# V projections of a fused attention and spectral-filter kernel placed straight behind the K projections of their x block

## The chip, the cores and the metric

The kernel runs on one core of a Trainium2 chip. A core has a TensorE for matmuls (PE in the profile; its weight loads are PEld), a VectorE (DVE), a ScalarE (ACT), a GpSimd (POOL) and a SyncE (SP), which here only issues DMAs. Matmuls write to PSUM, eight banks of 128 x 512 float32 values; everything else lies in SBUF. The metric is the device time of one execution in microseconds, and lower is better.

## The reference

Two independent halves are computed and joined along the last axis: a spectral filter on `A_x`, and softmax attention with 32 heads of 20 channels on `B_x`. Sequence length 2048, model width 640, bf16.

```
def _A_ref(x, w_r, w_i):                 # x (1, 2048, 640)
    X = rfft2(x as float32); X = X * (w_r + 1j * w_i)
    return irfft2(X).astype(bfloat16)
def _B_ref(x, wqkv, wo):                 # 32 heads, 20 channels each
    q, k, v = split(x @ wqkv)
    p = softmax(q @ k.T * 20 ** -0.5)
    return (p @ v) @ wo
return concatenate([a, b], axis=-1)
```

## The kernel before, in words

**A planner that writes the order.** The program is built by a list scheduler in the kernel file. The class `KB` holds work of several kinds, steps a clock of its own (`self.now`, in ns, with a planned duration for each operation), and at each step gives each engine the best thing that its own books show as ready. What comes out is a fixed instruction order for each engine, with semaphore waits put in where data or buffers need them. The planned times are not measured times; on the chip each engine simply follows its list.

**Attention.** There are 32 units (`UNITS`): a block of 512 queries (`qc`) and a group of four heads (`g`). A unit has 64 score tiles: 16 key tiles (`kt`, 128 keys each) times four heads (`j`). Unit 0 is query block 0 with head group 0, unit 1 is query block 1 with head group 0, units 2 and 3 are head group 1, and so on. A score tile is a matmul with 32 rows of the array (line 808), transposed: keys on the partitions, 512 queries along the free axis.

- ScalarE takes two tiles at once, out of a set of two PSUM banks (banks 0,1 and 2,3 in turn), and writes exp into one slot of a ring of seven slots (line 1389). A slot is free again when both its tiles have been multiplied by V.
- VectorE takes other tiles, four to a batch, and works out exp by arithmetic on the bits of float16 (lines 933, 961, 962, 963). It takes none before 30 us of planned time (`EARLY`, `MAXE`).
- P·V (line 1048) adds 21 x 512 per head into one PSUM bank for a unit. One column of V is ones, which gives the sums of the softmax.

TensorE's choice at each planned step is `step_pe1`: first the next two score tiles for ScalarE (`try_act_fill`); then P·V if at least eight tiles wait, or if the ring is full; then background groups (`try_bg`). A background group may start only if there is room before ScalarE would run dry, and only one is in work on TensorE at a time; its matmuls ("chunks") may be interleaved with scores. As long as ScalarE has not begun (`act_started` is False) or no score tile is ready, the room is unlimited. Background groups use PSUM banks 4 to 7, and all eight banks before ScalarE has begun.

**The background groups of the front** (`jobs_B`). x comes in four blocks of 512 rows (`i` or `kc`), and the smaller the priority number the earlier a group goes, if it is ready:

| group | line | matmuls | planned | priority |
|---|---|---|---|---|
| transposes of x block `i`, four groups | 584 (eviction 590) | 20 of 128 columns | 240 or 360 ns each group | 10 i + t2 |
| K of head group 0, block kc | 606 (eviction 614) | 5 of 512 | 1080 ns | 10 kc + 5 |
| Q(0,0), query block 0 of head group 0 | 606 (614) | 5 of 512 | 1080 ns | 5.5 |
| V of heads 0 to 7, two x tiles `2*k2`, `2*k2+1` | 682 (eviction 688) | 10 of 160 | 700 ns | 500 + k2 |
| Q(0,1), query block 1 of head group 0 | 606 (614) | 5 of 512 | 1080 ns | 550 |
| K and Q of head group 1 | 606 (614) | 5 of 512 | 1080 ns | 605 to 650 |
| K and Q of the other heads ("packed") | 635 (eviction 647) | 5 of 512 | 1080 ns | 1000 and up |

A transpose's eviction may run on ScalarE before the first scores and on VectorE at any time; K and Q are evicted by VectorE. A K block holds four key tiles, so it feeds 16 score tiles of a unit; two V groups together cover the key tiles of one block. Score tiles are taken in order, and no later unit is begun while the present one has tiles that aren't ready, except by VectorE.

Loads are issued by SyncE in this order: identity, x block 0 in two halves, the K and Q weights of head groups 0 and 1, a bias, and then, once the first half of x has landed, x block 1, the V weights, x blocks 2 and 3, the remaining K weights and the remaining Q weights.

**What else runs.** When all of x is transposed, GpSimd begins to fold `A_x` for the spectral filter (lines 1588 to 1595, eight rounds), and its results go through DRAM. The filter's matmuls (lines 1688, 1745, 1833, 1860) are released by planned times between 200 and 770 us and fill TensorE's gaps beside the attention. After a unit, its sums go through DRAM, GpSimd multiplies (line 1100), and the output projection (line 1194) follows when a query block is complete.

Of the kernel before, what the change touches and what calls it, by code (L numbers as in the profile page):

```python
# [293 lines left out]
class KB:  # L294
# [275 lines left out]
    def jobs_B(self):  # L570
        ps, psb = self.ps, self.psb
        J = {}
        for i in range(4):
            for t2 in range(2):
                for gi, cbs in enumerate(((0, 1, 2), (3, 4))):
                    n = len(cbs)
                    pe = []
                    for ci, c in enumerate(cbs):
                        for tt in range(2):
                            def mk(bank, ci=ci, c=c, tt=tt, i=i, t2=t2):  # L580
                                o = psb[:, bank, (ci * 2 + tt) * 128:(ci * 2 + tt) * 128 + 128]
                                in_ = self.xn[i][:, 2 * t2 + tt, c * 128:(c + 1) * 128]
                                idn = self.ident
                                return lambda e: e.transpose(o, in_, idn)
                            pe.append((mk, 60.0, [("xn", i, 2 * t2 + tt), ("ident",), ("xz", i), ("z", "D", 0)]))

                    def mkev(bank, cbs=cbs, n=n, i=i, t2=t2):
                        o = self.xT[:, cbs[0]:cbs[0] + n, i * 512 + t2 * 256: i * 512 + t2 * 256 + 256]
                        in_ = psb[:, bank, 0:n * 256].rearrange("p (c s) -> p c s", c=n)
                        return lambda e, en: (e.copy(o, in_) if en == "act" else e.tensor_copy(o, in_))  # L590
                    ev = [(mkev, 0.52 * n * 256 + 70, [("z", "A", 0)], [("xT", i, t2, gi)], [], True)]
                    J[("xT", i, t2, gi)] = Job("xT", 10.0 * i + t2, pe, ev)

        def xk(i):
            return [("xT", i, t2, gi) for t2 in range(2) for gi in range(2)]
# [31 lines left out]
        def packed(which, c, kc, sb, free):  # L627
            pe = []
            col = which * 640
            for cc in range(5):  # L630
                def mk(bank, cc=cc):
                    o = ps[:, bank, :]
                    l = self.wqkv[:, cc, col + c * 128: col + (c + 1) * 128]
                    r_ = self.xT[:, cc, kc * 512:(kc + 1) * 512]
                    return lambda e: e.matmul(o, l, r_, start=(cc == 0), stop=(cc == 4))  # L635
                wks = []
                if 128 * c < 160:
                    wks.append((("wq0", "wk0")[which],))
                if 128 * c + 128 > 160:
                    wks.append((("wq", "wk")[which],))  # L640
                pe.append((mk, 216.0, wks + [("z", "B", 0), ("z", "A", 0)] + xk(kc) + (free if cc == 0 else [])))

            def mkev(bank):
                o = self.stg[sb][:, kc * 512:(kc + 1) * 512]
                in_ = ps[:, bank, :]
                sc = (QSCALE, 1.0)[which]
                return lambda e, en: e.tensor_scalar(o, in_, sc, None, ALU.mult)  # L647
            ev = [(mkev, 610.0, [("z", "C", 0)], [("stg", which, c, kc)], [("stgb", sb, kc)], False)]
            return Job("pk%d" % which, 0.0, pe, ev)
# [3 lines left out]
        for n_, (which, c) in enumerate(order):  # L653
# [3 lines left out]
                for kc in (range(2, 4) if (which, c) == (0, 0) else range(4)):  # L657
                    j = packed(which, c, kc, sb, free)
# [12 lines left out]
        for m in range(4):  # L671
            for k2 in range(8):
                pe = []
                for i in range(2):
                    kt = 2 * k2 + i
                    for c in range(5):
                        def mk(bank, c=c, kt=kt, i=i, m=m):
                            o = ps[:, bank, i * 160:(i + 1) * 160]
                            l = self.xT[:, c, kt * 128:(kt + 1) * 128]
                            r_ = self.wqkv[:, c, 1280 + m * 160: 1280 + (m + 1) * 160]  # L680
                            st = (c == 0 and i == 0)
                            return lambda e: e.matmul(o, l, r_, start=st, stop=(c == 4), skip_group_check=True)  # L682
                        pe.append((mk, 70.0, [("wv",), ("z", "B", 0), ("z", "A", 0)] + xk(kt // 4)))

                def mkev(bank, k2=k2, m=m):
                    o = self.V[:, 2 * k2:2 * k2 + 2, m, 0:168].rearrange("p k (h e) -> p k h e", e=21)[:, :, :, 0:20]
                    in_ = ps[:, bank, 0:320].rearrange("p (k h e) -> p k h e", k=2, h=8)
                    return lambda e, en: (e.copy(o, in_) if en == "act" else e.tensor_copy(o, in_))  # L688
                ev = [(mkev, 405.0, [], [("V", m, 2 * k2), ("V", m, 2 * k2 + 1)], [], True)]
                j = Job("V", 500.0 + k2 if m == 0 else 1000.0 + 20.0 * m - 5 + k2 * 0.1, pe, ev)  # L690
                j.rel = 0.0 if m == 0 else self.VJ0 + self.VJ1 * (m + 0.125 * k2)
                J[("V", m, k2)] = j
        for j in J.values():
# [587 lines left out]
    def try_bg(self, room):  # L1281
        if any(J.nxt < len(J.pe) for J in self.flight):
            return False
        banks = self.POOLB if self.act_started and self.ua < NU else (4, 5, 6, 7, 0, 1, 2, 3)
        if self.act_started and not self.tail() and (self.n_dve_banks() >= len(self.POOLB) - 1 or (self.want_pv() and sum(1 for b in self.POOLB if self.bank_owner[b] is None) < 2)):
            return False
        best = None
        for J in self.jobs:
            if not J.pe or not self.eligible(J):
                continue  # L1290
            if best is not None and (best.prio, best.seq) <= (J.prio, J.seq):
                continue
            if min(sum(c[1] for c in self.part(J)), self.BMIN) + self.SW > room or not self.ready(J):
                continue
            best = J
        if best is None:
            return False
        fb = best.bank
        for b in banks if fb is None else ():
            if self.bank_owner[b] is None and self.P.peek("pe", w=[("ps", b)]) <= self.now:  # L1300
                fb = b
                break
        if fb is None:
            return False
        self.jobs.remove(best)
        best.bank = fb
        self.bank_owner[fb] = "bg"
        self.flight.append(best)
        self.emit_chunk(best)
        return True  # L1310
# [799 lines left out]
```

## Time and profile before

| | before |
|---|---|
| time, median of 3 runs | 796.37 us (796.0 to 797.88) |
| profiled execution, span | 797.3 us |
| mean granted TensorE clock | 0.998 |
| exponentials on ScalarE (two tiles each) | 823 |
| score tiles on VectorE | 403 |
| DMA traffic, mean | 61 GB/s |

The page of the profile gives the busy time of each engine as a share of the span, the chain of work that ended last, and the costliest groups of instructions with the idle time before them and who ended it. The timeline gives instructions in order of time, merged where the same line repeats; a bracket at the end tells how long the engine sat idle before it, and which engine and line ended the wait. TensorE's busy time is taken from matmul durations that overlap, so a stretch can look full while more would fit in. The windows view gives, for a stretch of time, the busy time of each engine, the granted clock and the DMA traffic.

### The profile page before, as it was taken

The numbers are of one execution on the slowest core, as the hardware profiler recorded it, in microseconds if no ns is written. First come the engines' busy times: TensorE is split into PE (matmuls) and PEld (weight loads), VectorE is DVE, ScalarE is ACT, GpSimd is POOL, SyncE is SP. The second block draws the span as 40 slices with busy tenths as digits, with TensorE's granted clock in tenths as the row PEclk, the third lists the DMA queues.
The fourth block names the chain that finished last, engine by engine and source line by source line (L and its number), as shares of the span: only waits on it lengthen the run. The fifth ranks groups of instructions, "written<-read, shape, count | busy, mean of one in ns | idle before, by whom it ended". The sixth has DMA issues, their size and how long they took to land.

```text
span 797.3 us, 15245 instructions
## 1 busy us (share of the span) xinstructions
PE 763.8 (96%) x6107; PEld 239.3 (30%) x6107; DVE 698.2 (88%) x1079; ACT 765.1 (96%) x836; POOL 138.7 (17%) x141
## 2 busy tenths in 40 slices
PE   8999999999989999999999999999998999999997
PEld 4422424233222222233233332222222322322333
DVE  4687899889998998999999999989899889989884
ACT  5789999999999999999999999999999999999995
POOL 7895800000100012103013010000000000000000
PEclk9999999999999999999999999999999999999999
DMA  9213221030154112212012112020200102111101
GB/s 296 79 44 104 82 72 46 23 69 20 45 159 153 59 64 60 70 44 57 6 36 61 44 36 107 19 72 19 72 20 16 35 30 73 52 36 35 51 21 53
DMA packets 42860, 48.65 MB, mean 61 GB/s; under 512 B 16454, under 2 KB 36168, under 8 KB 41760
## 3 DMA queue, kind: packets, MB, share of 16 engines
q1 hardware_dynamic: 42016, 46.32, 19.4%
q0 software_dynamic: 768, 1.32, 0.6%
q8 instruction: 49, 0.80, 0.4%
q14 instruction: 27, 0.22, 0.1%
HBM read 32.53 MB, written 8.36 MB: 51 GB/s over the span
## 4 chain that ended last, share of the span: by engine, by line
ACT 74%; PE 16%; DVE 8%; SPq 1%; issue 0%; DMA 0%
ACT arena L1389 74%; PE ps L808 5%; PE ps L1048 3%; DVE arena L962 2%; DVE arena L933 2%; PE ps L1688 1%; PE ps L606 1%; DVE arena L961 1%; PE ps L1194 1%; PE ps L635 1%; PE ps L1745 1%; PE ps L682 1%; DVE arena L963 1%; PE ps L564 1%; SPq L472 1%
## 5 line engine op out<-in xcount | busy, mean ns | idle before, releaser
L1389 ACT ACTIVATE arena<-ps 128x1024 f16<-128x1024 f32 x823 | 757.8, 1118 | 15.3 <-PE ps L1048 9.8
L808 PE MATMUL ps<-arena 32*128 32x512 bf16 x2048 | 324.6, 385 | 23.5 <-ACT arena L1389 18.8
L933 DVE TENSOR_SCALAR arena<-ps 128x512 int16<-128x512 f32 x403 | 269.7, 684 | 46.0 <-PE ps L808 42.8
L1048 PE MATMUL ps<-arena 128*32 128x512 f16 x2451 | 211.6, 385 | 1.4 <-DVE arena L963 0.7
L808 PEld LDWEIGHTS ps<-arena 32*128 32x128 bf16 x2048 | 79.5, 91 | 321.6 <-ACT arena L1389 299.0
L1100 POOL TENSOR_TENSOR arena<-arena 128x512 bf16<-128x512 f32 x30 | 41.7, 1391 | 543.4 <-DMA arena<-rd 543.4
L962 DVE TENSOR_TENSOR arena<-arena 128x2048 f16<-128x2048 f16 (+2 forms) x102 | 129.9, 1274 | 2.2
L961 DVE TENSOR_SCALAR arena<-arena 128x2048 uint16<-128x2048 uint16 (+2 forms) x102 | 73.9, 725 | 1.9
L963 DVE TENSOR_SCALAR arena<-arena 128x2048 uint16<-128x2048 uint16 (+2 forms) x102 | 73.6, 722 | 0.4
L1048 PEld LDWEIGHTS ps<-arena 128*32 128x32 bf16 x2451 | 45.9, 94 | 87.7 <-issue 65.9
L1833 PE MATMUL ps<-arena 128*128 128x512 bf16 (+1 forms) x192 | 56.8, 386 | 0.0
L635 PE MATMUL ps<-arena 128*128 128x512 bf16 x170 | 50.0, 384 | 0.3 <-DVE arena L688 0.3
L1688 PE MATMUL ps<-arena 128*128 128x512 bf16 x160 | 46.8, 384 | 0.9 <-DVE arena L933 0.9
L1745 PE MATMUL ps<-arena 128*128 128x322 bf16 (+1 forms) x198 | 38.0, 303 | 0.2 <-DVE arena L1776 0.2
L1860 PE MATMUL ps<-arena 128*128 128x320 bf16 (+1 forms) x192 | 37.1, 303 | 0.4 <-DVE arena L933 0.3
L1776 DVE TENSOR_TENSOR arena<-ps,arena 128x644 bf16<-128x644 f32 (+1 forms) x34 | 27.9, 822 | 3.7 <-PE ps L1745 3.1
L682 PE MATMUL ps<-arena 128*128 128x160 bf16 x320 | 30.5, 234 | 0.0
L1194 PE MATMUL ps<-arena 128*128 128x320 bf16 (+1 forms) x152 | 28.4, 302 | 0.1
L1079 DVE COPY arena<-ps 128x512 f32<-128x512 f32 (+1 forms) x33 | 21.9, 667 | 5.5 <-PE ps L1048 5.5
L647 DVE TENSOR_SCALAR arena<-ps 128x512 bf16<-128x512 f32 x34 | 23.3, 684 | 3.1 <-PE ps L635 3.1
L682 PEld LDWEIGHTS ps<-arena 128*128 128x128 bf16 x320 | 21.1, 98 | 11.3 <-issue 10.1
L688 DVE CAST arena<-ps 128x320 bf16<-128x320 f32 x32 | 15.4, 485 | 6.1 <-PE ps L682 6.0
(72 smaller groups left out, 361.3 us busy)
## 6 DMA issues: line engine op xcount, KB each, us to landing
arena<-ct SPq DMA_DIRECT2D x8, 1024.0 KB
arena<-rd SPq DMA_DIRECT2D x120, 64.0 KB
out_dram<-arena SPq DMA_DIRECT2D x32, 160.0 KB
arena<-arena SPq DMA_DIRECT2D x42, 80.0 KB
arena<-in_A_x_dram SPq DMA_DIRECT2D x16, 160.0 KB
xs<-arena SPq DMA_DIRECT2D x16, 160.0 KB
arena<-xs SPq DMA_DIRECT2D x2, 1280.0 KB
arena<-arena SPq DMA_DIRECT2D x105, 20.0 KB
```

The source lines that it names most:

```text
L635: return lambda e: e.matmul(o, l, r_, start=(cc == 0), stop=(cc == 4))
L682: return lambda e: e.matmul(o, l, r_, start=st, stop=(c == 4), skip_group_check=True)
L808: return e.matmul(self.ps[:, bank, :], self.KT[32 * j:32 * j + 32, g, kt * 128:(kt + 1) * 128], self.QT[32 * j:32 * j + 32, g, qc * 512:(q ...
L933: return e.tensor_scalar(o, in_, 0.0, 31744.0, ALU.max, ALU.min)
L961: (lambda e, en: e.tensor_scalar(Gu, Iu, 0x3FF, 0x3800, ALU.bitwise_and, ALU.bitwise_or), 100 + 0.26 * 512 * n, ik, [("G", b), ("G2", b)], ...
L962: (lambda e, en: e.tensor_tensor(Gf, If, Gf, ALU.mult), 125 + 0.52 * 512 * n, ik + [("G", b)], [("G2", b)], [], "p3"),
L963: (lambda e, en: e.tensor_scalar(Iu, Iu, 0x7C00, 0x0008, ALU.bitwise_and, ALU.bitwise_or), 100 + 0.26 * 512 * n, [("G2", b)], ik, [], "p4"),
L1048: inst = e.matmul(self.ps[32 * j:32 * j + 32, bank, :], v_, p_, start=s_, stop=False, tile_position=(0, 32 * j), skip_group_check=True)
L1389: self.put("act", lambda e: e.activation(o, in_, AF.Exp, bias=ACT_BIAS, scale=ACT_SCALE), 0.8333 * 512 * n + 60.0, r=[("ps", b) for b in b ...
L1688: return lambda e: e.matmul(o, l, r_, start=(t == 0), stop=(t == 7))
L1745: return lambda e: e.matmul(o, lhs, r_, start=st, stop=sp)
L1833: return lambda e: e.matmul(o, l, r_, start=(n == 0), stop=(n == 7))
```

## The change

The change touches two places of the planner and no instruction's form. The V groups for heads 0 to 7 get priorities between those of the K group of their x block and of the next block's transposes: 7.0 and 7.1 for block 0, 17.2 and 17.3 for block 1, 27.4 and 27.5, 37.6 and 37.7. They serve the first units' P·V, which empties the ring of exponentials. The second place is the choice of background groups: from the moment that Q(0,0) has begun until the first scores have been issued, groups with more than 400 ns of planned matmuls are passed over, so that none of them stands in front of the first scores.

```
@@ -687,7 +687,7 @@
                     in_ = ps[:, bank, 0:320].rearrange("p (k h e) -> p k h e", k=2, h=8)
                     return lambda e, en: (e.copy(o, in_) if en == "act" else e.tensor_copy(o, in_))
                 ev = [(mkev, 405.0, [], [("V", m, 2 * k2), ("V", m, 2 * k2 + 1)], [], True)]
-                j = Job("V", 500.0 + k2 if m == 0 else 1000.0 + 20.0 * m - 5 + k2 * 0.1, pe, ev)
+                j = Job("V", 10.0 * (k2 // 2) + 7.0 + k2 * 0.1 if m == 0 else 1000.0 + 20.0 * m - 5 + k2 * 0.1, pe, ev)
                 j.rel = 0.0 if m == 0 else self.VJ0 + self.VJ1 * (m + 0.125 * k2)
                 J[("V", m, k2)] = j
         for j in J.values():
@@ -1287,6 +1287,8 @@
         best = None
         for J in self.jobs:
             if not J.pe or not self.eligible(J):
+                continue
+            if not self.act_started and self.jB[("Q0", 0, 0)].nxt and sum(c[1] for c in J.pe) > 400:
                 continue
             if best is not None and (best.prio, best.seq) <= (J.prio, J.seq):
                 continue
```

More of the change, by code (lines that the diff above doesn't have):

```diff
@@ L689, in jobs_B @@
                 ev = [(mkev, 405.0, [], [("V", m, 2 * k2), ("V", m, 2 * k2 + 1)], [], True)]
-                j = Job("V", 500.0 + k2 if m == 0 else 1000.0 + 20.0 * m - 5 + k2 * 0.1, pe, ev)
+                j = Job("V", 10.0 * (k2 // 2) + 7.0 + k2 * 0.1 if m == 0 else 1000.0 + 20.0 * m - 5 + k2 * 0.1, pe, ev)
                 j.rel = 0.0 if m == 0 else self.VJ0 + self.VJ1 * (m + 0.125 * k2)
@@ L1289, in try_bg @@
             if not J.pe or not self.eligible(J):
+                continue
+            if not self.act_started and self.jB[("Q0", 0, 0)].nxt and sum(c[1] for c in J.pe) > 400:
                 continue
```

## The prediction

> **What bounds the kernel now.** I read the page's busy times first, then the chain that ended last, then ScalarE's timeline for the first 60 us, then TensorE's for the stretch in which ScalarE stands still, and last the windows of the granted clock.
>
> From the page, the busy shares and the start of the chain by engine and line:
>
> ```profile
> PE 763.8 (96%) x6107; PEld 239.3 (30%) x6107; DVE 698.2 (88%) x1079; ACT 765.1 (96%) x836; POOL 138.7 (17%) x141
> ...
> ACT 74%; PE 16%; DVE 8%; SPq 1%; issue 0%; DMA 0%
> ```
>
> ScalarE (ACT) carries three quarters of the chain. TensorE's 96% is no second bound: the mean matmul of 512 columns stands at 385 ns, but ten of them on L606 below take 2.33 us, so the next starts after (2.33 - 0.38) / 9 = 0.216 us; the ends overlap. ScalarE is idle for 797.3 - 765.1 = 32.2 us in all, and its timeline says where the early part of that lies (start, length, what; in brackets the idle time before and who ended it):
>
> ```profile
> 13.58 6.52 ACT L1389 ACTIVATE arena<-ps 128x1024 f16<-128x1024 f32 x7 [0.82 <-PE ps L808]
> 24.82 24.44 ACT L1389 ACTIVATE arena<-ps 128x1024 f16<-128x1024 f32 x26 [4.71 <-PE ps L1048]
> 49.67 1.02 ACT L1389 ACTIVATE arena<-ps 128x1024 f16<-128x1024 f32 x1 [0.41 <-PE ps L808]
> 51.96 1.02 ACT L1389 ACTIVATE arena<-ps 128x1024 f16<-128x1024 f32 x1 [1.27 <-PE ps L808]
> 54.23 6.52 ACT L1389 ACTIVATE arena<-ps 128x1024 f16<-128x1024 f32 x7 [1.24 <-PE ps L1048]
> ```
>
> Seven exponentials run, exactly the seven slots of the P ring, and then ScalarE waits 4.71 us for a P·V matmul (L1048) to empty a slot. P·V needs V. TensorE's timeline shows when V came:
>
> ```profile
> 8.69 2.33 PE L606 MATMUL ps<-arena 128*128 128x512 bf16 x10
> 10.86 1.28 PE L584 MATMUL ps<-arena 128*128 128x128 bf16 x20
> 11.98 1.24 PE L606 MATMUL ps<-arena 128*128 128x512 bf16 x5
> ...
> 18.65 0.82 PE L606 MATMUL ps<-arena 128*128 128x512 bf16 x3
> 19.40 0.39 PE L808 MATMUL ps<-arena 32*128 32x512 bf16 x2
> 19.72 0.61 PE L606 MATMUL ps<-arena 128*128 128x512 bf16 x2
> 20.26 0.39 PE L808 MATMUL ps<-arena 32*128 32x512 bf16 x2
> 20.58 0.73 PE L584 MATMUL ps<-arena 128*128 128x128 bf16 x10
> 21.17 1.56 PE L682 MATMUL ps<-arena 128*128 128x160 bf16 x20
> 22.57 1.24 PE L606 MATMUL ps<-arena 128*128 128x512 bf16 x5
> 23.74 1.04 PE L1048 MATMUL ps<-arena 128*32 128x512 f16 x14
> ```
>
> The first V (L682) stands at 21.17, behind all transposes (L584) and three K groups of unit 0; another K group follows, and only then P·V. The five matmuls at 11.98 are a K group of head group 1: the last evictions of the transposes just issued were still running, so the K block of x block 1 could not be meant. It stands in front of the first scores at 13.15.
>
> A third fact, from the windows (length, busy PE, PEld, DVE, ACT, POOL, granted clock, DMA share, GB/s):
>
> ```profile
> 50.50:53.50 3.00, 3.00 (x10) 0.49 (x8) 1.19 (x3) 1.22 (x2) 3.00 (x4) 0.50 0.01 3
> ```
>
> TensorE ran this stretch at half clock, and ScalarE lost the 0.41 + 1.27 + 1.24 = 2.9 us around it.
>
> **What the Trainium skill says.** "TensorE: Matmul & The Clock Gate", section "Back-to-back issue gap", gives N / 2.4 + 2.5 ns between warm matmuls: 216 ns at 512 columns, as worked out above. The same page, "What's actually happening", says that the clock falls to half after an idle window of about 3.4 us; the trace agrees with the length (half clock for some 3.4 us), and no run yet shows what counts as idle. "SBUF — State Buffer", section "SBUF: two separate sides", says that VectorE and GpSimd lock one port pair against each other for a whole instruction; the trace agrees: the multiply L962 takes 2.30 us at 35.50 and 45.25, beside GpSimd's fold, and 1.22 us after 100 us.
>
> **The change, part by part.** *The priorities of V for heads 0 to 7.* They go from 500 + k2 to 7, 17, 27, 37 for the pairs of x blocks 0 to 3, so each pair runs behind the K group (5, 15, 25, 35) of its block and ahead of the next block's transposes (10, 20, 30). No instruction is added or removed. The first pair cannot run before its weights are there; that load is fourth in a queue of 0.69 + 0.41 + 0.66 + 0.82 = 2.6 MB, and the traffic by microsecond sums to 2.4 MB at 10 us and 2.8 MB at 11, so it lands near 11 us (an estimate). The planner books its bytes at 270 per ns from a 4.0 us issue and another 1.9 us, about 12.2 us. V therefore does not wait for data, and it comes behind the first scores, near 13.5 us.
>
> *What that frees.* Twenty V matmuls start to start take 22.57 - 21.17 = 1.4 us; in the 0.6 us that a pair of scores leaves per exponential (starts 0.93 apart, 0.32 of it for scores) they are done after three exponentials. Eight tiles are then multiplied by V after the fourth, before the ring's seven slots are full. The 4.71 us goes.
>
> *The rule against long groups.* Between the first matmul of Q(0,0) and the first scores no group planned at over 400 ns starts: K, Q and V groups (1080 and 700 ns) wait, transposes do not. This removes the K group at 11.98. The scores still need a PSUM bank that ScalarE's transpose eviction frees at 11.40 + 1.37 = 12.77. So from 13.15 the first scores can move to 12.8 at the earliest: 0 to 0.4 us, I take 0.2.
>
> *What it moves to the front instead.* K for tiles 32 to 63 now queues behind V and P·V. TensorE's demand up to the last K block of unit 0: V of three blocks 6 x 0.7 = 4.2; three K groups 3 x 1.08 = 3.2; 40 transposes 2.2 (20 are 1.12 start to start); P·V for 24 exponentials, six batches of eight matmuls at about 0.5, 3.0: 12.7 us. Supply: the block must be complete some three exponentials ahead (two sets filled ahead, one eviction of 0.75), so 21 x 0.61 = 12.8 us. It balances with nothing left for groups that can't be split, turns that hold no whole chunk, and waits for evictions. A tenth lost is 1.3 us. Walking the list in order I find the K block of tile 32 about 0.9 us late; for tile 48 the walk gives anything between on time and 3.5 us late. I take 1.5 us of new ScalarE waits, with 0.9 and 4.4 as ends.
>
> *What costs nothing.* Moving the group at 11.98 and Q(0,1) back: head group 1 is due only at tile 128, and 44 tiles are done near 37 us, so some 30 us lie before it. V's evictions (0.49 us each) on VectorE: it is busy 3.9 of the 6.5 us from 13.6 to 20.1.
>
> *What shifts.* The last transposes move from 21 us to about 33, and GpSimd's fold, which waits for them, with them. Two of its eight rounds lay before the first VectorE batch of four score tiles; they now lie beside later ones. A batch beside the fold took 0.85 + 2.30 + 1.22 = 4.4 us against 2.6 alone; one more such batch costs VectorE 1.8 us, part of which is idle time. I take 0, and 0.5 us of end time as the other bound.
>
> *From ScalarE time to end time.* ScalarE does 823 x 2 = 1646 of the 2048 tiles, VectorE the rest from 30 us on, which the change does not move. A microsecond of ScalarE saved at the front is worth 1646 / 2048 = 0.80 us at the end. Sum: (0.2 + 4.7 - 1.5) x 0.80 = 2.7 us, so 796.4 - 2.7 = 793.7 us.
>
> **The rivals.** *The half-clock stretch goes too.* It followed stretches in which TensorE stood idle (48.0 to 48.3, 49.9 to 50.3) behind slow VectorE evictions. With one K group more left over there is more for TensorE at that time; against it, the fold still slows VectorE there. Worth 2.9 x 0.80 = 2.3: 791.4 us.
>
> *A wait that takes the place of the one removed.* If the last transposes and their evictions come behind V and behind the first VectorE score tiles at 30 us, the K block for tile 48 comes 3.5 us late, the new waits are 4.4 us, and (0.2 + 4.7 - 4.4) x 0.80 = 0.4 remains: 796.0 us. For it speaks that demand and supply of TensorE balance so closely; against it, that ScalarE's own wait gives TensorE full speed.
>
> *Slower.* TensorE starves in a new place (the whole list is planned anew from the first microsecond), a second half-clock stretch costs 2.3, and the later fold 0.5: 796.0 + 2.8 = about 799 us. For it: a stretch of this kind exists already, and later exponentials show scattered waits of up to 1.4 us per 10 us. Against it: ScalarE sits at 10.00 of 10 us in most windows from 110 to 780, so there is little that can get worse.
>
> **How the numbers follow.** The forecast 0.32, without the half-clock stretch 0.20, the wait moved 0.28, slower 0.20. A change of 0.3% is 2.4 us, so faster holds the first two, 0.52; same 0.28; slower 0.20. The range reaches from below the second case, 790.0, with 1.4 us for what else moves, to 798.5, past the third, and leaves out most of the slower case.
>
> **What would show it.** Right: the first L682 close behind the first scores near 13.5; no ScalarE idle time of over 2 us ended by L1048 before 30 us; the first exponential near 13.4; small waits ended by L808 at about 28 and 36 us; the fold's start near 33 us. Wrong: a wait of 3 us or more for L808 before unit 0 ends (the rival of the moved wait), or V waiting for its weights, or ScalarE's idle time after 40 us grown by more than 2 us.

## The result, and the profile after

| | before | after |
|---|---|---|
| time, median of 5 runs each | 797.07 us (796.0 to 798.48) | 806.33 us (805.05 to 809.12) |
| ratio, with its 95% interval | | 1.0117 (1.0092 to 1.0143) |
| profiled execution, span | 797.3 us | 803.2 us |
| exponentials on ScalarE | 823 | 829 |
| score tiles on VectorE (L933) | 403 | 392 |

The kernel became 1.2% slower. Lines past 1289 have moved by two: the exponential is now L1391, the filter's first matmul L1690. From the page of after, the busy times, the chain by engine and the two rows that do the exponentials (the last column is the idle time before them and what ended most of it):

```profile
PE 756.5 (94%) x6052; PEld 239.5 (30%) x6105; DVE 689.2 (86%) x1059; ACT 771.5 (96%) x842; POOL 145.2 (18%) x141
...
ACT 52%; PE 39%; DVE 7%; issue 1%
...
L1391 ACT ACTIVATE arena<-ps 128x1024 f16<-128x1024 f32 x829 | 764.2, 1105 | 15.0 <-PE ps L808 10.8
...
L933 DVE TENSOR_SCALAR arena<-ps 128x512 int16<-128x512 f32 x392 | 262.2, 683 | 61.3 <-PE ps L808 58.5
```

ScalarE stands idle for 803.2 - 771.5 = 31.7 us, nearly as long as before, 32.2 us. What the change won at the front was thus lost again elsewhere. And ScalarE is busy for 6.4 us more (771.5 against 765.1), since it has six exponentials more to do where VectorE did eleven tiles fewer. These two terms make up the 5.9 us between the two profiled executions; the medians lie further apart, by 9.3 us, because the profiled execution of after was its fastest, and that of before (799.17 us) was slower than all five of its runs. TensorE's share of the chain rose from 16% to 39%; in e3 below, which is faster than before, it is 27%, so the share alone says little.

The front itself went largely as foreseen. TensorE's timeline of after shows V straight behind the first scores:

```profile
12.83 0.39 PE L808 MATMUL ps<-arena 32*128 32x512 bf16 x4 [0.68 <-ACT arena L590]
13.16 1.14 PE L682 MATMUL ps<-arena 128*128 128x160 bf16 x14
```

And ScalarE's timeline of after:

```profile
13.26 14.77 ACT L1391 ACTIVATE arena<-ps 128x1024 f16<-128x1024 f32 x16 [0.48 <-PE ps L808]
29.03 6.10 ACT L1391 ACTIVATE arena<-ps 128x1024 f16<-128x1024 f32 x7 [1.00 <-PE ps L808]
38.36 6.52 ACT L1391 ACTIVATE arena<-ps 128x1024 f16<-128x1024 f32 x7 [3.23 <-PE ps L808]
45.52 1.02 ACT L1391 ACTIVATE arena<-ps 128x1024 f16<-128x1024 f32 x1 [0.64 <-PE ps L808]
46.77 30.93 ACT L1391 ACTIVATE arena<-ps 128x1024 f16<-128x1024 f32 x33 [0.23 <-PE ps L808]
```

The wait of 4.71 us for a P·V is gone. Waits for scores of 1.00, 3.23 and 0.64 us, 4.9 us together, stand in its place; but the half-clock stretch at 50 us is gone too (the windows of after give a granted clock of 1.00 from 50.5 to 53.5 us). So up to 100 us after is ahead; e4 below shows that most of this lead can be chance. Where it falls behind is seen by counting: two tiles for each exponential on ScalarE and one for each L933 on VectorE, from the windows view of these two rows, each window from 0 to the time given.

| tiles done by | 60 us | 100 | 120 | 200 | 240 | 260 | 400 | 500 | 780 |
|---|---|---|---|---|---|---|---|---|---|
| before | 97 | 196 | 252 | 470 | 581 | 634 | 1012 | 1271 | 2037 |
| after, against before | +5 | +9 | +3 | -3 | -1 | -8 | -15 | -14 | -16 |

Before does 2037 / 780 = 2.6 tiles per us, so 16 tiles are 6.1 us, which is the difference of the two spans (5.9). Two stretches carry it: 100 to 200 us, and from 240 to 400 us. Both lie far from the edit.

### The profile page after: what moved, and what is told of

Same layout as the page of the kernel before. It is cut to its first block, busy times and chain, and to the rows that moved or that the text cites. A ratio compares the mean times of both kernels' runs of the same rounds, so it can differ in the third digit from the quotient of the medians.

```text
span 803.2 us, 15169 instructions
## 1 busy us (share of the span) xinstructions
PE 756.5 (94%) x6052; PEld 239.5 (30%) x6105; DVE 689.2 (86%) x1059; ACT 771.5 (96%) x842; POOL 145.2 (18%) x141
## 3 DMA queue, kind: packets, MB, share of 16 engines
q1 hardware_dynamic: 42016, 46.32, 19.1%
## 4 chain that ended last, share of the span: by engine, by line
ACT 52%; PE 39%; DVE 7%; issue 1%
ACT arena L1391 51%; PE ps L808 14%; PE ps L1048 9%; PE ps L635 4%; PE ps L682 3%; PE ps L1835 2%; DVE arena L933 2%; PE ps L1690 2%; DVE arena L962 2%; PE ps L606 1%; PE ps L1194 1%; PE ps L1862 1%; DVE arena L961 1%; DVE arena L963 1%; PE ps L1747 1%
## 5 line engine op out<-in xcount | busy, mean ns | idle before, releaser
L1391 ACT ACTIVATE arena<-ps 128x1024 f16<-128x1024 f32 x829 | 764.2, 1105 | 15.0 <-PE ps L808 10.8
L808 PE MATMUL ps<-arena 32*128 32x512 bf16 x2048 | 323.6, 385 | 27.1 <-ACT arena L1391 22.7
L933 DVE TENSOR_SCALAR arena<-ps 128x512 int16<-128x512 f32 x392 | 262.2, 683 | 61.3 <-PE ps L808 58.5
L808 PEld LDWEIGHTS ps<-arena 32*128 32x128 bf16 x2048 | 79.4, 91 | 323.3 <-ACT arena L1391 302.1
L1100 POOL TENSOR_TENSOR arena<-arena 128x512 bf16<-128x512 f32 x30 | 44.9, 1498 | 548.1 <-DMA arena<-rd 548.1
L962 DVE TENSOR_TENSOR arena<-arena 128x2048 f16<-128x2048 f16 (+1 forms) x99 | 126.8, 1280 | 1.9
L963 DVE TENSOR_SCALAR arena<-arena 128x2048 uint16<-128x2048 uint16 (+1 forms) x99 | 74.4, 751 | 0.2
L961 DVE TENSOR_SCALAR arena<-arena 128x2048 uint16<-128x2048 uint16 (+1 forms) x99 | 72.1, 729 | 2.1
L1835 PE MATMUL ps<-arena 128*128 128x512 bf16 (+1 forms) x176 | 52.8, 386 | 2.4 <-issue 1.6
L635 PE MATMUL ps<-arena 128*128 128x512 bf16 x155 | 46.0, 383 | 2.5 <-issue 1.8
L1690 PE MATMUL ps<-arena 128*128 128x512 bf16 x144 | 43.1, 387 | 3.7 <-issue 3.6
```

Source lines behind the costliest of these rows:

```text
L808: return e.matmul(self.ps[:, bank, :], self.KT[32 * j:32 * j + 32, g, kt * 128:(kt + 1) * 128], self.QT[32 * j:32 * j + 32, g, qc * 512:(q ...
L933: return e.tensor_scalar(o, in_, 0.0, 31744.0, ALU.max, ALU.min)
L961: (lambda e, en: e.tensor_scalar(Gu, Iu, 0x3FF, 0x3800, ALU.bitwise_and, ALU.bitwise_or), 100 + 0.26 * 512 * n, ik, [("G", b), ("G2", b)], ...
L962: (lambda e, en: e.tensor_tensor(Gf, If, Gf, ALU.mult), 125 + 0.52 * 512 * n, ik + [("G", b)], [("G2", b)], [], "p3"),
L963: (lambda e, en: e.tensor_scalar(Iu, Iu, 0x7C00, 0x0008, ALU.bitwise_and, ALU.bitwise_or), 100 + 0.26 * 512 * n, [("G2", b)], ik, [], "p4"),
L1391: self.put("act", lambda e: e.activation(o, in_, AF.Exp, bias=ACT_BIAS, scale=ACT_SCALE), 0.8333 * 512 * n + 60.0, r=[("ps", b) for b in b ...
```

## The experiments

All ratios are against the kernel before, run beside it on the same chip (its medians there: 798.35 to 798.9 us). A "draw" is the list that the planner happens to write, and a "redraw" another one, got by moving a planned number that means nothing for the work. Below, "first pair", "priorities" and "rule" are parts of the change, put into the kernel before.

### The parts of the change, and a redraw of the kernel before

Four runs. The rule alone and the priorities alone are the two hunks of the change. The first pair gives the early priority to the two V groups of x block 0 only:

```
# e3_first_pair, against before
-  Job("V", 500.0 + k2 if m == 0 else ...
+  Job("V", (7.0 + k2 * 0.1 if k2 < 2 else 500.0 + k2) if m == 0 else ...
# e4_before_other_latency: a planned latency of the kernel before, and nothing else
-    L_DVE = 140.0
+    L_DVE = 141.0
```

> The rule against long groups alone, V priorities as before. Theory A (the front's new order itself costs: V pushes the K groups and the fold back): 0 to -0.5 us against before, since V stays where it was, and 400 to 406 score tiles on VectorE. Theory B (any edit of the front makes the planner write another list for the following 700 us, and the list of before is a favourable one among many): +2 to +9 us, though the first 60 us are nearly unchanged. Theory C (the K group of head group 1 that the rule takes out of an idle stretch is missed later): +3 us or more, and the loss shows in TensorE waits before 120 us.

> The V priorities alone, without the rule. Theory A: as the changed kernel, +8 to +10 us, with the waits for scores near 28 and 36 us. Theory B: the same gain of tiles at 90 us as the changed kernel (about 8), and an end anywhere from 0 to +9 us. Theory C: 0 us or faster.

> Only the two V groups of x block 0 go ahead (priorities 7.0 and 7.1), the other six stay at 500 and up, no rule. Theory A: the 4.7 us wait goes and no wait for scores of over 1 us comes in its place, the fold starts before 30 us, and the kernel is 3 to 6 us faster than before. Theory B: ahead by 8 to 14 tiles at 90 us, but an end of -4 to +5 us, because the rest of the list is new. Theory C: faster by 3 us or more, since the K group of head group 1 stays in its place.

> The kernel before with one planned figure changed: the planner books a VectorE result 141 ns after its end in place of 140. No priority and no rule is touched. Theories A and C: within 1 us of before, 400 to 405 score tiles on VectorE. Theory B: +2 to +9 us, fewer score tiles on VectorE than 403, tile counts equal to before's within 3 up to 60 us.

| | time, us | ratio (95%) | tiles against before at 100 | 200 | 260 | 780 us |
|---|---|---|---|---|---|---|
| e1 rule alone | 806.24 | 1.0111 (1.0063 to 1.0160) | +7 | -4 | -4 | -12 |
| e2 priorities alone | 799.72 | 1.0027 (1.0013 to 1.0040) | +10 | +4 | +5 | 0 |
| e3 first pair | 793.40 | 0.9945 (0.9928 to 0.9962) | +20 | +14 | +16 | +11 |
| e4 redraw of before | 800.90 | 1.0033 (1.0017 to 1.0049) | +7 | +5 | +7 | -6 |

Three things follow. In these four runs the slow-down is in the rule: alone it costs about what the whole change does, and the priorities, with the same front as after (waits of 1.00 and 3.23 us), end 0.27% above before. Second, the later V groups are what breaks the front. ScalarE's timeline of e3 shows no wait for a K block:

```profile
13.34 13.86 ACT L1389 ACTIVATE arena<-ps 128x1024 f16<-128x1024 f32 x15 [0.82 <-PE ps L808]
29.20 18.49 ACT L1389 ACTIVATE arena<-ps 128x1024 f16<-128x1024 f32 x20 [2.01 <-PE ps L1048]
47.86 33.10 ACT L1389 ACTIVATE arena<-ps 128x1024 f16<-128x1024 f32 x36 [0.17 <-PE ps L1048]
```

One pair of V groups sets P·V going; the other three blocks' V stay behind the K groups, and one wait of 2.01 us for the ring is left. e3 does 829 exponentials and 392 tiles on VectorE, just as after does, in 11 us less: the smaller share of VectorE is not by itself what makes a kernel slow. It has a price, though. VectorE does 388 to 396 tiles in all twelve kernels here with V early, and 398 to 405 in seven of the eight with V as before (394 in e10). In e2 ScalarE stands idle for 3.8 us less than in before (28.4 against 32.2) and is busy for 3.7 us more (768.8 against 765.1), so nothing is left of the gain. Why VectorE falls behind with V early is not shown.

Third, e4 changes nothing at the front and one number by 0.7%, and takes 0.33% longer. The list that the planner draws is new behind the first place that differs, and the one in the kernel before is a good draw. In e4 that place lies late: the order of TensorE's weight loads, by line, is that of before up to 387 us, and e4 is 3 tiles ahead of before at 400 us and 6 behind at 780. Its 7 tiles at 100 us are therefore not of the list. Its first exponential came at 12.99 us and not at 13.58, and it has no half clock at 50 us, where the same list in before has (the line of before stands in the prediction):

```profile
50.50:53.50 3.00, 3.00 (x30) 0.84 (x28) 2.48 (x5) 2.41 (x3) 3.00 (x3) 1.00 0.01 3
```

A count of tiles from one profile against that of before thus carries some 7 tiles of chance, and of the 9 that after is ahead at 100 us few are sure.

### How much is the draw: the same kernels with another start of the filter

`FT0` is the planned time at which the filter's matmuls begin to be released. It is moved by 0.1 or 0.3 us; the front stays as it is in each kernel. The order of TensorE's weight loads stays too, up to 390 us in e5, 326 in e6, 336 in e7 and 392 in e8.

```
-    FT0 = 200000.0
+    FT0 = 200100.0     # e5 (after), e7 (before)
+    FT0 = 200300.0     # e6 (rule alone), e8 (first pair)
```

> The changed kernel with one planned figure of the filter changed: its first group is released at 200.1 us of planned time in place of 200.0. The order up to about 200 us is the changed kernel's own. Theory A' (the change and above all its rule lose the time at the front, before 200 us): 804 to 808 us, as the changed kernel. Theory B (the loss is in the list that the planner happens to write for the later part): the tile counts at 160 us are the changed kernel's within 2, and the end differs from it by 2 us or more, probably downward, 799 to 804 us, since the changed kernel lies at the slow end of the lists seen so far.

> The rule alone, with the filter's first release at 200.3 us of planned time. Theory C (the rule itself costs): 804 to 808 us, as the rule alone. Theory B: 798 to 804 us, with more than 3 us between this and the rule alone, tile counts equal up to about 200 us.

> The kernel before with the filter's first release at 200.1 us of planned time in place of 200.0. Theories A' and C: within 1 us of before. Theory B: +1 to +6 us against before, with an order equal to before's up to about 200 us, and fewer score tiles on VectorE than 403.

> Only the first pair of V groups ahead, no rule, with the filter's first release at 200.3 us of planned time. Theory A': 792 to 795 us, as the first pair alone, since the front is the same. Theory B: slower than the first pair alone by 1 to 8 us, 795 to 801 us.

| | time, us | ratio (95%) |
|---|---|---|
| e5 after | 810.85 | 1.0125 (1.0060 to 1.0189) |
| e6 rule alone | 801.72 | 1.0038 (1.0023 to 1.0052) |
| e7 before | 801.29 | 1.0041 (1.0025 to 1.0057) |
| e8 first pair | 800.64 | 1.0034 (1.0018 to 1.0051) |

A tenth of a microsecond in a planned time costs the kernel before 0.41%, and 0.3 us takes the whole gain of the first pair away: e8 is +12 tiles ahead at 400 us, as e3 is, and 3 behind at 780. A difference of 0.3 or 0.4% between two lists is therefore no sign that the edit between them does anything. After stays 1.2% slower, but e5 has its list up to 390 us, so what after loses before that, e5 loses too; it is no second draw of that part. The rule alone doesn't stay 1.1% slower, so something in e1 is not the rule itself.

Nor is all of a difference the list. Each run has a mean granted clock of its own, and of the twenty runs of e7 the five at 0.997 or more have a median of 799.25 us, where such runs of before have 798.14: 0.14% of the 0.41%. The rest goes with half clock (last section).

### The filter's first matmul stands before its data

TensorE's timeline of after around 240 us:

```profile
238.76 0.39 PE L808 MATMUL ps<-arena 32*128 32x512 bf16 x2 [0.53 <-ACT arena L1391]
241.14 0.71 PE L1690 MATMUL ps<-arena 128*128 128x512 bf16 x2 [1.99 <-issue]
241.78 0.61 PE L808 MATMUL ps<-arena 32*128 32x512 bf16 x2
242.32 1.03 PE L1690 MATMUL ps<-arena 128*128 128x512 bf16 x2
```

TensorE stands for 1.99 us before the first matmul of the filter's first stage, and all scores queued behind it stand too; and the two L1690 behind the next scores take 1.03 us, where such a pair takes 0.59 to 0.60 us in e9. After's profile names no releaser ("issue"). The timeline of e1 has a wait at the same matmul and names it, a load of a table of constants; that after waits for the same load is an inference:

```profile
236.63 0.82 PE L1690 MATMUL ps<-arena 128*128 128x512 bf16 x3 [1.36 <-DMA arena<-ct]
```

The planner books these loads at 270 bytes per ns. If the books are too fast, slower books should put the matmul later and take the stand away:

```
# e9_after_later_filter, against after: planned rate of the filter's two loads
-        rate = 90.0 if name == "spread" else 270.0
+        rate = 90.0 if name == "spread" else 215.0 if name in ("ld_xA", "ld_tab") else 270.0
```

> The changed kernel, with the filter's x and table loads booked by the planner at 215 bytes per ns in place of 270, so that the filter's first matmuls stand about 2 us later in TensorE's list and find their table landed. The order up to about 235 us is the changed kernel's. Theory D (the changed kernel loses about 10 tiles between 238 and 260 us, because TensorE stands 2 us before the filter's first matmul, and then runs at half clock): no wait of over 0.5 us ahead of L1690's first matmul, no half-clock stretch between 238 and 250 us, 52 tiles or more between 240 and 260 us where the changed kernel has 44, and 801 to 804 us. Theory B alone (chance of the later list): tile counts at 240 us equal, and any end from 799 to 810 us.

It took 803.19 us, ratio 1.0050 (1.0034 to 1.0066), where after had 1.0117. The windows view (length, busy PE, PEld, DVE, ACT, POOL with their counts, granted clock, DMA share, GB/s), first of after:

```profile
238.00:241.50 3.50, 0.99 (x7) 0.32 (x5) 1.93 (x5) 2.54 (x3) 0.00 (x0) 1.00 1.00 354
241.50:245.00 3.50, 3.50 (x20) 0.58 (x18) 1.90 (x3) 2.05 (x2) 0.00 (x0) 0.52 1.07 430
240.00:260.00 20.00, 18.56 (x127) 4.78 (x134) 14.45 (x22) 17.28 (x20) 1.26 (x1) 0.91 0.34 125
```

then of e9:

```profile
238.00:241.50 3.50, 2.97 (x28) 0.76 (x25) 3.21 (x5) 3.50 (x5) 0.00 (x0) 1.00 0.96 345
241.50:245.00 3.50, 3.50 (x28) 1.01 (x28) 3.21 (x7) 3.50 (x5) 0.00 (x0) 1.00 1.09 434
240.00:260.00 20.00, 20.00 (x156) 5.14 (x155) 18.24 (x29) 20.00 (x23) 1.26 (x1) 1.00 0.34 127
```

The DMA engines are full in both (share about 1.0), so the loads come no sooner. In e9 TensorE works through scores meanwhile, ScalarE has no idle time from 240 to 260 us, and the clock stays at 1.00. In after TensorE is busy 0.99 of 3.5 us, and the next 3.5 us run at a granted clock of 0.52. This is the idle window of which the Trainium skill speaks ("TensorE: Matmul & The Clock Gate", section "What's actually happening"); the trace of after agrees with it, though TensorE was not idle for the whole of the window. How idle a window must be the runs don't show: the stand of 1.63 us in e14 was followed by no half clock, and other half-clock stretches followed shorter stands (last section). At 260 us e9 is 9 tiles ahead of after, at 780 us 5 tiles. The times differ by 0.67% of after's 1.17%; since e9 is a redraw as well, a part of that can be the draw. After in another draw, e16 below, stands there for 0.88 us only and comes to 1.0059, close to e9.

e5, with after's list up to there, has the same stand, 1.88 us, and 10.2 us of half clock behind it. In the three kernels with the rule alone (e1, e6, e14) it is 1.36, 1.48 and 1.63 us, and the clock stays at 1.00 there. None of the eleven kernels without the rule stands there longer than 1.02 us (before: 0.86). That the rule leads to longer stands by more than the draw is not shown: e12 and e18 below have the rule and stand under 0.3 us.

### The later fold

In after GpSimd begins the fold at 33.02 us and ends it near 110, where before began at 21.49 and ended near 97. From 100 to 120 us before has no GpSimd at all beside VectorE, after has 9.3 us, and VectorE did 12 tiles in before against 8 in after. So I held the fold back in the kernel before:

```
# e10_before_fold_late
         J = Job("fold", 0.0, after=[...], post=lambda J: self.fold_x())
+        J.rel = 34000.0
```

> The kernel before, with GpSimd's fold held back until 34 us of planned time, about where the changed kernel has it. V and the rule as before. Theory A2 (the later fold takes VectorE's time, 5 score tiles of it between 100 and 120 us): 7 to 9 score tiles on VectorE between 100 and 120 us where before has 12, and 0 to 2 more than before between 34 and 60 us. End by theory B: +1 to +6 us; by A2 alone: +1 to +2 us.

798.64 us, ratio 1.0001 (0.9983 to 1.0020). On the chip the first rounds did not move (the first L1588 of e10 starts at 21.67): GpSimd has nothing else to do and runs them when their data is there. The later rounds did move, presumably since their loads are issued later, and the fold ends near 110 us as in after. From 100 to 120 us VectorE does 9 tiles, about as in after. But e3, whose fold ends at 98.4 us, also does 9 there, so the three tiles fewer than in before need not be the fold's. e10 is 14 tiles ahead of before at 100 us, with no half-clock stretch at 50 us, and 9 at 120, and nothing of the late end shows in the time. Nothing here makes it the cause. A late start by itself was not tried.

### The first pair with the rule, and a second setting of the first pair

e11 is the first pair with three planned numbers set anew, to see whether its gain stands in another list (one picked, as the shortest on the planner's own clock among some tens); e12 adds the rule to the first pair of e3.

```
# e11_first_pair_retuned, against e3
-    L_PE = 215.0
+    L_PE = 216.0
-    FT0 = 200000.0
-    FT1 = 770000.0
+    FT0 = 201000.0
+    FT1 = 766000.0
```

> The first pair of V groups ahead and no rule, with three planned figures changed (the filter's release from 201 to 766 us in place of 200 to 770, a TensorE result booked 216 ns after its end in place of 215), picked as the shortest list on the planner's own clock among some tens. If the planner's own clock tells good lists from bad ones: 790 to 793 us, at or below the first pair alone. If it doesn't: 793 to 800 us.

> The first pair ahead together with the rule. Theory C2 (the rule costs in every list, in small waits of ScalarE between 100 and 200 us and in a wait before the filter's first matmul): 1.2 us or more of ScalarE idle time between 100 and 200 us where the first pair alone has 0.7, a wait of over 1 us at L1690's first matmul, and 3 to 7 us slower than the first pair alone. Theory B: within -2 and +6 us of the first pair alone, with no such pattern.

e11 took 793.45 us, 0.9939 (0.9919 to 0.9958); e12 798.03 us, 0.9993 (0.9979 to 1.0006). With the rule e3's gain is gone, and the front is the same: in e12 the first exponential starts at 13.09 instead of 13.34, the waits behind it are those of e3, and both are 20 tiles ahead at 100 us. At 200 us e12 is 9 ahead and e3 14; at 400 us 2 and 12.

### Six pairs with and without the rule

Six more runs give before, rule, priorities, after, first pair, and first pair with rule once more, all with another planned latency:

```
# e13 to e18
-    L_PE = 215.0
+    L_PE = 216.0
```

> The kernel before with a TensorE result booked 216 ns after its end in place of 215. Theory B (draw of the list): between 0 and +5 us against before. Theory C2 (the rule alone costs, other edits are neutral): within 1 us.

> The rule alone, with 216 ns. Theory C2: 3 to 9 us slower than the same figure without the rule (the run before this one). Theory B: between -4 and +6 us against it.

> The V priorities alone, with 216 ns. Theory B: 798 to 804 us, anywhere around the V priorities alone with 215 ns. Theory C2: within 1 us of the V priorities alone (about +2 us against before).

> The changed kernel, with 216 ns. Theory C2: 3 to 9 us slower than the V priorities alone with 216 ns. Theory B: between -4 and +6 us against it. If TensorE's first filter matmul stands before its table's landing again, a wait of 1 us or more there and a stretch at half clock behind it.

> Only the first pair of V groups ahead, no rule, with a TensorE result booked 216 ns after its end in place of 215. Theory B: 791 to 799 us. If the front's gain (20 tiles at 100 us) carries to the end in most lists: 791 to 796 us.

> The first pair of V groups and the rule, with 216 ns. Theory C2: 3 to 9 us slower than e17. Theory B: between -4 and +6 us against it.

| V groups, `L_PE` | without the rule | with the rule | the rule costs | tiles from 100 to 200 us, without and with |
|---|---|---|---|---|
| as before, 215 | 1 | 1.0111 (e1) | 1.11% | 274, 263 |
| as before, 216 | 1.0015 (e13) | 1.0069 (e14) | 0.54% | 272, 264 |
| all four blocks, 215 | 1.0027 (e2) | 1.0117 (the change) | 0.90% | 268, 262 |
| all four blocks, 216 | 1.0031 (e15) | 1.0059 (e16) | 0.28% | 268, 260 |
| first pair, 215 | 0.9945 (e3) | 0.9993 (e12) | 0.48% | 268, 263 |
| first pair, 216 | 0.9962 (e17) | 1.0001 (e18) | 0.39% | 268, 264 |

The intervals of these ratios are 0.1 to 0.5% to each side. The rule is slower in all six, by 0.62% on average, and by 0.28 to 1.11%. The draw alone has moved the kernel before by 0.15 to 0.41%, so no single pair proves much, and the two kernels of a pair are two lists. The draws without a partner don't speak for the rule either: e6, with it, lies at 1.0038 within the redraws of before (1.0015 to 1.0041), and e8, without it, at 1.0034 above e12 and e18. What speaks for it is that all six pairs go one way, and the tiles with them. The first pair is faster than before in three of its four draws (e3, e11, e17) and not in e8. All four blocks' V early, without the rule, are 0.3% slower than before in both draws, no more than a redraw of before is.

Where the rule's cost shows first is 100 to 200 us. There the kernel with the rule does 4 to 11 tiles fewer in every pair, at 2.6 tiles per us some 1.5 to 4 us, where profiles of one and the same list differ by 2 tiles at most (before 274, e7 274, e4 272). The windows view of that stretch, first of before, then of e1, the same kernel with the rule:

```profile
100.00:200.00 100.00, 99.35 (x849) 33.24 (x847) 90.91 (x142) 99.71 (x110) 5.09 (x4) 1.00 0.19 46
100.00:200.00 100.00, 99.46 (x835) 33.18 (x835) 88.43 (x135) 97.95 (x107) 5.09 (x4) 1.00 0.19 46
```

ScalarE does three exponentials fewer, VectorE is busy for less time, and TensorE's busy time doesn't tell the two apart. The waits view of ScalarE for the stretch (who waits for whom: us in all, times, longest), of before:

```profile
ACT arena L1389 <- PE ps L1048: 0.2, 1, 0.2
```

of e1:

```profile
ACT arena L1391 <- PE ps L1048: 1.7, 5, 0.6
```

The wait for P·V in this stretch is 1.1 to 1.7 us in the nine kernels with the rule and 0 to 0.7 us in the eleven without. It is a handful of waits of 0.2 to 0.6 us each, and it explains some 0.5 to 1.5 us of a cost of 2 to 9 us. Why P·V comes late there is not shown. TensorE loads weights for 4 to 9 more matmuls of packed K and Q groups (L635) there with the rule, in each pair (97 in e1, 90 in before); whether P·V waits for these was not tested.

## Why the prediction was wrong

**The front: right in its steps, with one term too small.** V came at 13.16 us without waiting for its weights; the 4.71 us went; the fold began at 33.02. The rule gave 0.34 us (I took 0.2): the first exponential begins 0.82 us after ScalarE's last copy in the eleven kernels without the rule and 0.48 us after it in the nine with it, as the bracket of e2 shows beside that of after above:

```profile
13.12 14.77 ACT L1389 ACTIVATE arena<-ps 128x1024 f16<-128x1024 f32 x16 [0.82 <-PE ps L808]
```

That e2 starts earlier than after all the same, at 13.12 against 13.26, is no merit of its list: the start alone varies by 0.6 us between kernels with the same one (12.99 in e4, 13.58 in before). The new waits came at 28 and 35 us, where the walk had put them, but they sum to 1.00 + 3.23 + 0.64 = 4.9 us and not 1.5. The rival of the moved wait had this right with its 4.4: the last transposes (L584, 30.5 to 32.8 us) and the last K block (L606, from 33.7) lie behind V and the first VectorE scores, and the scores themselves (37.9) behind one more V group. e3 shows how to avoid it, by leaving V of the later blocks behind K.

**The half-clock stretch at 50 us did go,** as the first rival had it. This may be luck: e4 lost it too, with the order of before. It was also priced too high. The prediction counted 2.9 us of waits around it, and e4, with no half clock there, still has 0.41 + 0.62 + 0.39 = 1.4 us of them; and the second stand of TensorE that it read there lasted 0.21 us (from 50.14), not 0.4. With the measured front and this term as it was priced, the sum of the prediction would have been (0.3 + 4.7 - 4.9 + 2.9) x 0.80 = 2.4 us faster; the priorities alone, with this very front, are at +5 tiles by 260 us and at 0 by 780.

**The step that failed is the last one, from ScalarE time to end time,** with the sentences that rest on it: that moving the K group at 11.98 costs nothing, that VectorE does its part "which the change does not move", and that ScalarE sits at 10.00 of 10 us later on, so that little can get worse there. They take the list behind the front as given. It isn't: the exchange rate of 0.80 holds only while nothing later moves, and everything later was drawn anew. In the profiled execution VectorE's part fell from 403 tiles to 392, ScalarE's busy time grew by 6.4 us, and its idle time fell by 0.5 us where the sum had 3.4. The runs show three costs behind the front:

- The filter's first matmul stood for 2 us, by the evidence of e1 before its load, and was followed by 3.4 us of half clock. Taking the stand away gave back 0.67% of the 1.17% (e9, a part of which can be the draw).
- The rule cost 0.28 to 1.11% in six pairs, though all it does by itself is keep one K group of 1.08 us out of a slot before the first scores, which gains 0.34 us there. Where the group is done instead, and what it pushes away, stays open; the first sign is the 4 to 11 tiles fewer and the wait for P·V between 100 and 200 us. The stand before the filter is part of this cost in the pair with the change.
- The draw itself: 0.15 to 0.41% for edits of before that mean nothing, half clock in some of their runs included.

These overlap, and the runs don't split the 1.17% into shares that add up.

**The rival on the slower side had the mechanism in part.** It said that TensorE would starve in a new place since the list is planned anew, with a second half-clock stretch, and both came at 240 us. Its 2.8 us were sized by the stretch at 50 us alone; 9 us came. Its chance of 0.20 was argued down by the full windows from 110 us on, and that was the mistake: full windows show how much a list has to lose, not that it is safe. The later fold, the other part of that rival, cost nothing that shows (e10, as far as its late end goes). The 4.4 us that the prediction took for a VectorE batch beside the fold hold for the first two batches: in before the multiply L962 took 2.30 us at 35.50 and 45.25, but 1.22 at 73.33, also beside the fold, and there it was GpSimd's L1594 that took longer, 1.85 us and not 0.86.

**The signs I had named** spoke in part: a wait of 3 us or more for L808 before unit 0 ends was to show the forecast wrong, and 3.23 us stood there. ScalarE's idle time after 40 us was to grow by more than 2 us, and did not: 18.8 us before, 19.1 after. No sign watched what ScalarE had to do.

## What to carry to other kernels

Where a planner draws the whole instruction order, an edit at the front is also a redraw of everything behind it: price the redraw with neutral edits of both versions (here 0.15 to 0.41%) before a smaller difference is credited to the edit, and count the work done up to a few times instead of reading idle time alone. Profile one list twice before a count is trusted: the same order stood 7 tiles apart here. In an in-order queue the first consumer of a load needs a margin in the plan, since everything behind it stands with it and the clock may fall afterwards. And when early work frees a ring, move only as much of it as sets the ring going: one pair of V groups gave 0.4 to 0.6% in three of four draws (one of the three picked from many), all four pairs gave nothing.

## What the runs showed of the hardware

The half clock comes in multiples of one length: 3.4 us in after (from 241.5), 6.8 us in e18, 10.2 us in e5 (from 243.1), 13.7 us in e7 and e10. Its places are not fixed by the list: before has it from 50.3 us, and e4, with the same order of weight loads up to 387 us, has none there. e5 has three times as much as after behind the same stand.

Nor does TensorE's busy time in the profile tell where it comes. Of the 3.40 us ahead of the stretch in before (46.90 to 50.30) TensorE was busy for 2.81, and no stand in them was longer than 0.30 us; in e4 the same work (46.30 to 49.70) shows 2.80 of 3.40, with full clock behind it. In e14 TensorE was busy for only 1.77 of 3.40 us around its stand (233.30 to 236.70), and no half clock followed.

What half clock costs shows in e7. It and before are within one tile of each other at each of the times above up to 400 us (1012 both); then the profiled execution of e7 has half clock from 409 us, where before has none. The windows view of before:

```profile
409.00:419.00 10.00, 9.34 (x83) 3.06 (x77) 8.59 (x15) 10.00 (x12) 0.38 (x1) 1.00 0.03 5
```

and of e7:

```profile
409.00:419.00 10.00, 10.00 (x52) 2.32 (x48) 6.70 (x10) 6.68 (x7) 0.00 (x0) 0.50 0.01 2
```

At half clock ScalarE does 7 exponentials in 10 us instead of 12, though TensorE's busy time reads as full. e7's twenty runs reach from 797.95 to 809.78 us, and the mean granted clock goes with the time: 0.998 in the fastest, 0.986 at 804.89 us, 0.981 in the slowest (correlation -0.96). So half clock goes with most of that spread; where it lay in the runs without a profile is not known.
